# Order of the products in blocks two and three of the second MoE: two of layer one, then both halves of one of layer two

## The chip, the cores and the metric

One Trainium2 chip, one core. The metric is the device time of one execution in microseconds; the three runs of the kernel before took 2061.57 to 2063.62 us, with a median of 2063.37.

## What is computed

Sliding-window attention (4 x 8 heads, 576 positions, head size 64), then two feed-forward stages over the 2304 tokens of 512 values. The second one is the place of the change. Eight experts each have two layers, and their results are added with weights P that a Sinkhorn iteration over the gate's logits gives:

```python
for e in range(E):                      # E = 8, D = 512, F = 1024
    h = np.maximum(x @ w1[e], 0.0)      # layer one
    ye = h @ w2[e]                      # layer two
    out += P[:, e:e + 1] * ye
```

## The kernel before

The second MoE takes the tokens in three blocks of 768, each of two halves of 384 columns (HALF). Both layers are done as 2 x 2 block products with Strassen's scheme, seven products in place of eight, on sums and differences of the blocks. Every factor is split into a high and a low part, and a product of blocks is six matmuls with 384 moving columns (two parts of the contraction, and in each high x high, high x low, low x high; lines 122 to 124, the function mm3).

Blocks two and three run in one loop over m, from NQ = 16 to total - 1 = 47. I call one m a quad: it is half of an expert's F for one block, worked on as two pairs of slices of 128, so 16 quads make a block. A quad has 14 steps s; step(m, s) issues product p = s % 7 of layer one for pair s // 7 (g_product) and one half of a product of layer two of the quad before (y_product(m - 1, s): product s // 2, half dt = s % 2). In the texts g0 to g6 are the layer-one products of the first pair of a quad, g'0 to g'6 those of the second, and y is one half. Quad 16 has no layer-two products yet (old is false at m = 16; its first steps finish block one instead), quad 31's products of layer two follow a plain list of eight products (PLAIN), and those of quad 47 come after the loop, in last_quad. A manual schedule is declared ahead of this stage (line 859): every engine's work has the order in which the program issues it.

The seven products of layer one add up in three PSUM banks of a pair:

```python
    GP = [(0, "b11", 0), (1, "b21", 1), (5, "t2", 0), (4, "t1", 2), (6, "t3", 0), (2, "t4", 0), (3, "b22", 2)]
...
        o, b, bk = GP[p]
        first = p in (0, 1, 3)
```

The last number is the bank. With first a fresh bank is opened (one of four, in turn); otherwise the product adds onto what is there. Between two such products the bank's state is read out (g_evict): for p = 0 a ScalarE copy (line 939), p = 1 a VectorE sum (942), p = 2 a ScalarE copy (945), p = 4 a ScalarE copy called u3 and a VectorE sum with bank 2:

```python
            nc.scalar.copy(new_temp("u3", "m"), v1)
            c = v3 if inside else temps["u3"]
            nc.vector.tensor_add(c, v2, temps["u3"])
```

(lines 947 to 949), p = 5 a ScalarE Relu straight from the bank, p = 6 a VectorE sum (955). The results go through a Relu on ScalarE (line 1338) into R.

Layer two has four PSUM banks of its own, yb: two of them for each half dt. A product's result is added by VectorE to the sums acc in SBUF (line 1272, 128 x 384), before the next product on that bank.

Between these, step(m, s) issues for VectorE the scaling of R by the expert's weights (scaled, line 1212) and Strassen's sums (r_sum, lines 1217 to 1223), at s = 0 (t1), 2 (t3), 3 (t2), 5 (t4), and for ScalarE and GpSimd the splits in high and low parts (r_hi, line 1231; r_lo, line 1236), at s = 0, 2, 4, 5 and, for the next quad, 9, 12, 13. SP loads one weight block of layer one after each g product, in eight places (load_w1, line 763), and one of layer two at every odd step (w2_op, line 1248, nine places). x_switch changes the block's tokens at the end of a block.

Of the kernel before, what the change touches and what calls it, by code (L numbers as in the profile page):

```python
# [29 lines left out]
def attention_moe_moe2(  # L30
# [89 lines left out]
    def mm3(ps, lhs, rhs, first, last, **kw):  # L120
        (lh, ll), (rh, rl) = lhs, rhs
        nc.tensor.matmul(ps, lhsT=lh, rhs=rh, start=first, stop=False, **kw)  # L122
        nc.tensor.matmul(ps, lhsT=lh, rhs=rl, start=False, stop=False, **kw)  # L123
        nc.tensor.matmul(ps, lhsT=ll, rhs=rh, start=False, stop=last, **kw)  # L124
# [633 lines left out]
    def load_w1(j):  # L758

        n, p = divmod(j, 7)  # L760
        if NP <= n < NB * NP and j not in w1q:
            w = w1q[j] = p3.tile([P, 2, 2, P], F32R, name="w1o", tag="w1o", bufs=8)
            nc.sync.dma_start(raw(w), d_w1[n % NP][:, GP[p][0]])
# [160 lines left out]
    def g_product(n, p):  # L924
        o, b, bk = GP[p]
        first = p in (0, 1, 3)
        if first:
            gb[bk] = g_bank(f"g{bk}")
        w, x = slab[n][:, o] if n < NP else w1q.pop(7 * n + p), xop[b]
        for k in range(2):  # L930
            mm3(
                gb[bk][:, :HALF], (w[:, k, 0], w[:, k, 1]), (x[:, 0, k], x[:, 1, k]), first and k == 0, k == 1,
                skip_group_check=True,
            )

    def g_evict(p, rectify, inside=False):
        v1, v2, v3 = [gb[i][:, :HALF] if i in gb else None for i in (0, 2, 1)]
        if p == 0:
            nc.scalar.copy(new_temp("m1", "m"), v1)
        elif p == 1:  # L940
            c = v3 if inside else temps["m1"]
            nc.vector.tensor_add(c, v3, temps["m1"])
            rectify(c, 0, 0)
        elif p == 2:
            nc.scalar.copy(new_temp("u2", "u"), v1)
        elif p == 4:
# [3 lines that stand above are left out]
            rectify(c, 1, 1)  # L950
        elif p == 5:
            rectify(v1, 1, 0)
        elif p == 6:
            c = v2 if inside else temps["u2"]
            nc.vector.tensor_add(c, v2, temps["u2"])
            rectify(c, 0, 1)
# [15 lines left out]
    def x_switch(m, s):  # L972
        if m + 1 < NB * NQ and (m + 1) % NQ == 0:
            if s == 4:
                nc.vector.tensor_sub(xs["t1"], xs[0, 1], xs[0, 0])
            elif s == 6:
                nc.vector.tensor_sub(xs["t2"], xs[1, 1], xs["t1"])
            elif s == 8:
                nc.vector.tensor_sub(xs[0, 1], xs[1, 1], xs[0, 1])
            elif s == 11:  # L980
                nc.vector.tensor_sub(xs[1, 0], xs[1, 0], xs["t2"])
        elif m and m % NQ == 0 and s < 2:
            s += 14
        else:
            return
        order = LAST_SWITCH if m > NQ + 1 else SWITCH
        if s in order:
            nm, eng = order[s]
            src = {"b11": xs[0, 0], "b21": xs[1, 0], "b22": xs[1, 1], "t3": xs[0, 1], "t4": xs[1, 0]}.get(nm)
            x = xop[nm] = p2.tile([P, 2, 2, HALF], F32R, name=f"x{nm}", tag=f"x{nm}", bufs=1)  # L990
            split_sb(xs[nm] if src is None else src, x[:, 0], x[:, 1], (nc.vector, nc.gpsimd)[eng])
# [216 lines left out]
    def scaled(m, f, h):  # L1208

        pb = pbs[m // NQ, m % NQ // PER][:, h * HALF : (h + 1) * HALF]  # L1210
        r = R[m, f, h]
        nc.vector.tensor_mul(r, r, pb[:, None, :].to_broadcast([P, 2, HALF]))  # L1212

    def r_sum(m, nm):
        r = {(f, h): R[m, f, h] for f in range(2) for h in range(2)}
        if nm == "t1":
            nc.vector.tensor_sub(r[0, 0], r[0, 1], r[0, 0])  # L1217
        elif nm == "t2":
            nc.vector.tensor_sub(r[0, 0], r[1, 1], r[0, 0])
        elif nm == "t3":  # L1220
            nc.vector.tensor_sub(r[0, 1], r[1, 1], r[0, 1])
        elif nm == "t4":
            nc.vector.tensor_sub(r[1, 0], r[1, 0], r[0, 0])
# [14 lines left out]
    def r_op(m, nm):  # L1238
        r_hi(m, nm)
        if (m, nm) != (total - 1, "b21"):  # L1240
            r_lo(m, nm, nc.gpsimd)

    def w2_op(m, i):
        if m in PLAIN and i > 3:
            return
        o = (0, 2, 1, 3)[i] if m in PLAIN else YP[i][1]
        w = w2q[m, o] = wp.tile([P, 2, 2, 2 * P], F32R, name="w2o", tag="w2o", bufs=9)
        nc.sync.dma_start(raw(w), d_w2[m % NQ][:, o])

    def y_product(m, s):  # L1250

        i, dt = divmod(s, 2)
        b, op, bk, first, *dsts = (YP_LAST if m in PLAIN else YP)[i]
        if m < total - 1:
            bk %= 2
        ps = yb[2 * bk + dt]
        w, x = w2q[m, op], rop[m, b]
        ws = slice(dt * P, (dt + 1) * P)
        for a in range(2):
            mm3(  # L1260
                ps[:, :HALF], (w[:, a, 0, ws], w[:, a, 1, ws]), (x[:, 0, a], x[:, 1, a]), first and a == 0, a == 1,
                skip_group_check=True,
            )
        for dst in dsts:
            key = (m, dst, dt)
            if m % NQ == 0 and key not in touched:
                touched.add(key)
                if dt == 0:
                    acc[dst] = wp.tile([P, 2, HALF], F32, name=f"a{dst[0]}{dst[1]}", tag=f"a{dst[0]}{dst[1]}", bufs=1)
                nc.scalar.copy(acc[dst][:, dt], ps[:, :HALF])  # L1270
            else:
                nc.vector.tensor_add(acc[dst][:, dt], ps[:, :HALF], acc[dst][:, dt])  # L1272
# [54 lines left out]
    def step(m, s):  # L1327

        nonlocal wp
        if m < total:  # L1330
            pair, p = divmod(s, 7)

            def rectify(src, f, h):
                if pair == 0:
                    R[m, f, h] = (p3 if m % 2 else p2).tile(
                        [P, 2, HALF], F32, name=f"R{f}{h}", tag="Rb" if m % 2 else "Ra", bufs=4
                    )
                nc.scalar.activation(R[m, f, h][:, pair], src, AF.Relu)  # L1338

            g_product(2 * m + pair, p)  # L1340
            load_w1(7 * (2 * m + pair) + p + 8)
        old = NQ <= m - 1 < total
        if s in EARLY_OPS and m < total:
            scaled(m, *EARLY_OPS[s][1:])
        elif s in LATE_OPS and old and m < total:
            if s == 0:
                scaled(m - 1, 0, 1)
            if m - 1 not in PLAIN:
                r_sum(m - 1, LATE_OPS[s])
        if m < total:  # L1350
            g_evict(p, rectify)
        if s in EARLY_OPS and m < total:
            r_op(m, EARLY_OPS[s][0])
        elif s in LATE_SPLITS and old and m < total:
            if m - 1 not in PLAIN:
                r_op(m - 1, LATE_SPLITS[s])
            elif s == 2:
                r_op(m - 1, "t3")
        if old:
            if m - 1 not in PLAIN:  # L1360
                y_product(m - 1, s)
            else:
                for x in (s,) if s < 12 else (2 * s - 12, 2 * s - 11):
                    y_product(m - 1, x)
        if m < total:
            x_switch(m, s)
            if m > NQ:
                if s % 2:
                    w2_op(m, s // 2)
            elif s < 6:  # L1370
                values(before, (s,))
            elif s == 6:
                wps.close()
                wp = ctx.enter_context(tc.tile_pool(name="wpb", bufs=1))
            elif s % 2:
                for i in range(4) if s == 7 else (s // 2,):
                    w2_op(m, i)
            if s == 4 and m % PER == PER - 1 and m + 1 < total:
                load_pb((m + 1) // NQ, (m + 1) % NQ // PER)
        for d in range(2):  # L1380
            blk, q = divmod(m - d, NQ)
            if q == 0 and blk > 1:
                for dst, at in WHOLE:
                    for x in range(2):
                        if at + x == s + 14 * d:
                            turn_out(blk - 1, dst, x, yb[x] if dst == (1, 0) else None)
# [41 lines left out]
```

## Time and profile before

| | |
|---|---|
| median of three runs | 2063.37 us |
| lowest and highest run | 2061.57, 2063.62 us |
| span of the profiled execution | 2061.8 us |
| PE busy | 2025.9 us (98%) |
| VectorE busy | 1385.8 us (67%) |
| GpSimd busy | 1080.9 us (52%) |
| ScalarE busy | 955.5 us (46%) |
| DMA | 523.84 MB, 254 GB/s in the mean |

The page gives the span of the profiled execution and no other time for it; it lies 1.6 us under the median of the runs. In the timeline a matmul's start is recorded, its end is modelled, so consecutive matmuls overlap in the rows and the distance between starts is what counts.

### The profile page before, as it was taken

The numbers are of one execution on the slowest core, as the hardware profiler recorded it, in microseconds if no ns is written. First come the engines' busy times: TensorE is split into PE (matmuls) and PEld (weight loads), VectorE is DVE, ScalarE is ACT, GpSimd is POOL, SyncE is SP. The second block draws the span as 40 slices with busy tenths as digits, with TensorE's granted clock in tenths as the row PEclk, the third lists the DMA queues.
The fourth block names the chain that finished last, engine by engine and source line by source line (L and its number), as shares of the span: only waits on it lengthen the run. The fifth ranks groups of instructions, "written<-read, shape, count | busy, mean of one in ns | idle before, by whom it ended". The sixth has DMA issues, their size and how long they took to land.

```text
span 2061.8 us, 31510 instructions
## 1 busy us (share of the span) xinstructions
PE 2025.9 (98%) x10869; PEld 1854.1 (90%) x10869; DVE 1385.8 (67%) x2469; ACT 955.5 (46%) x1950; POOL 1080.9 (52%) x836
## 2 busy tenths in 40 slices
PE   7989999999999999999999999999999999999999
PEld 5767777887888899999999999999999999999999
DVE  7986755535147887777786766776676577667765
ACT  7665655434244444444444434444444444444443
POOL 4224343434358788788785444544454454445442
PEclk9999999999999999999999999999999999999999
DMA  7877877656649878887879878777786787877773
GB/s 208 280 211 252 265 221 195 193 164 204 209 159 327 295 307 319 320 310 287 313 297 343 285 254 256 259 259 256 253 273 228 260 256 260 258 256 235 270 260 106
DMA packets 290653, 523.84 MB, mean 254 GB/s; under 512 B 90416, under 2 KB 135104, under 8 KB 286400
## 3 DMA queue, kind: packets, MB, share of 16 engines
q1 hardware_dynamic: 290496, 521.85, 75.9%
q8 instruction: 87, 1.43, 0.3%
q14 instruction: 70, 0.57, 0.1%
HBM read 369.12 MB, written 152.64 MB: 253 GB/s over the span
## 4 chain that ended last, share of the span: by engine, by line
PE 69%; DVE 4%; issue 1%; ACT 1%; POOL 1%; DMA 0%; ACTq 0%; POOLq 0%; DVEq 0%
PE y L123 11%; PE y L124 11%; PE y L122 11%; PE g L122 11%; PE g L124 11%; PE g L123 11%; PE acc L122 1%; PE acc L123 1%; PE acc L124 1%; PE h L123 1%; PE h L122 1%; PE h L124 1%; DVE s L737 1%; DVE s L739 0%; DVE o L1044 0%
## 5 line engine op out<-in xcount | busy, mean ns | idle before, releaser
L1236 POOL TENSOR_TENSOR rb<-R,rb 128x768 fp32r<-128x768 f32 x95 | 214.0, 2253 | 345.3 <-ACT rb L1231 321.6
L1272 DVE TENSOR_TENSOR a<-y,a 128x384 f32<-128x384 f32 x420 | 232.4, 554 | 192.5 <-PE y L124 192.5
L1236 POOL TENSOR_TENSOR rt<-R,rt 128x768 fp32r<-128x768 f32 x121 | 230.4, 1915 | 138.5 <-ACT rt L1231 59.4
L114 POOL TENSOR_TENSOR w2a<-r,w2a 128x1024 fp32r<-128x1024 f32 x64 | 154.2, 2410 | 66.9 <-ACT w2a L113 66.9
L122 PE MATMUL g<-xt,w1o 128*128 128x384 f32 x512 | 173.8, 339 | 1.4 <-ACT u L947 1.0
L124 PE MATMUL g<-xt,w1o 128*128 128x384 f32 x512 | 172.6, 337 | 0.0
L123 PE MATMUL g<-xt,w1o 128*128 128x384 f32 x512 | 172.3, 337 | 0.0
L122 PE MATMUL y<-rt,w2o 128*128 128x384 f32 x496 | 168.1, 339 | 0.1
L123 PE MATMUL y<-rt,w2o 128*128 128x384 f32 x496 | 168.0, 339 | 0.0
L124 PE MATMUL y<-rt,w2o 128*128 128x384 f32 x496 | 167.4, 337 | 0.0
L1231 ACT ACTIVATE rt<-R 128x768 fp32r<-128x768 f32 x122 | 102.7, 842 | 134.7 <-DVE R L1217 84.0
L114 POOL TENSOR_TENSOR gl<-r,gh 128x512 fp32r<-128x512 f32 x64 | 83.0, 1297 | 155.9 <-ACT gh L113 130.9
L124 PE MATMUL y<-w2a,rl 128*128 128x512 f32 x384 | 150.1, 391 | 0.0
L123 PE MATMUL y<-w2a,rh 128*128 128x512 f32 x384 | 149.6, 390 | 0.2 <-POOL w2a L114 0.2
L122 PE MATMUL y<-w2a,rh 128*128 128x512 f32 x384 | 149.5, 389 | 0.0
L1212 DVE TENSOR_TENSOR R<-R,pb 128x768 f32<-128x768 f32 x128 | 138.5, 1083 | 5.4 <-ACT R L1338 3.9
L122 PE MATMUL y<-rb,w2o 128*128 128x384 f32 x408 | 138.3, 339 | 0.6 <-DVE a L1272 0.6
L123 PE MATMUL y<-rb,w2o 128*128 128x384 f32 x408 | 138.3, 339 | 0.0
L124 PE MATMUL y<-rb,w2o 128*128 128x384 f32 x408 | 137.6, 337 | 0.0
L122 PE MATMUL g<-xb,w1o 128*128 128x384 f32 x384 | 129.9, 338 | 0.0
L124 PE MATMUL g<-xb,w1o 128*128 128x384 f32 x384 | 129.5, 337 | 0.0
L123 PE MATMUL g<-xb,w1o 128*128 128x384 f32 x384 | 129.3, 337 | 0.0
(261 smaller groups left out, 5773.2 us busy)
## 6 DMA issues: line engine op xcount, KB each, us to landing
w1o<-d_w SPq DMA_DIRECT2D x448, 256.0 KB, 3.0
w2o<-d_w SPq DMA_DIRECT2D x218, 512.0 KB, 3.9
d_w<-w1a SPq DMA_DIRECT2D x32, 1792.0 KB, 11.6
d_w<-w2a SPq DMA_DIRECT2D x30, 1536.0 KB, 7.9
r<-in_moe_w_dram SPq DMA_DIRECT2D x64, 512.0 KB, 4.3
a<-d_in SPq DMA_DIRECT2D x48, 512.0 KB, 3.8
b<-d_out SPq DMA_DIRECT2D x48, 512.0 KB, 3.9
u<-in_moe_w_in_dram SPq DMA_DIRECT2D x16, 512.0 KB, 5.0
```

Of the source, the lines that this page charges most:

```text
L114: (eng or nc.gpsimd).tensor_sub(lo, src, raw(hi))
L122: nc.tensor.matmul(ps, lhsT=lh, rhs=rh, start=first, stop=False, **kw)
L123: nc.tensor.matmul(ps, lhsT=lh, rhs=rl, start=False, stop=False, **kw)
L124: nc.tensor.matmul(ps, lhsT=ll, rhs=rh, start=False, stop=last, **kw)
L737: nc.vector.tensor_sub(w1s[n][:, 2], w1s[n][:, 1], a11)
L1212: nc.vector.tensor_mul(r, r, pb[:, None, :].to_broadcast([P, 2, HALF]))
L1231: nc.scalar.activation(x[:, 0], R[m, f, h], AF.Copy)
L1236: eng.tensor_sub(x[:, 1], R[m, f, h], raw(x[:, 0]))
L1272: nc.vector.tensor_add(acc[dst][:, dt], ps[:, :HALF], acc[dst][:, dt])
```

## The change

In the loop over quads a step no longer issues one half of a layer-two product each time. At even s it issues none, at odd s both halves, s - 1 and s, of one product. For the quad with the plain list (m - 1 = 31) it is the same up to s = 11, and the last four halves come together at s = 13. Everything else in a step keeps its place.

```diff
--- before.py
+++ after.py
@@ -1356,12 +1356,13 @@
                 r_op(m - 1, LATE_SPLITS[s])
             elif s == 2:
                 r_op(m - 1, "t3")
-        if old:
+        if old and s % 2:
             if m - 1 not in PLAIN:
-                y_product(m - 1, s)
+                ys = (s - 1, s)
             else:
-                for x in (s,) if s < 12 else (2 * s - 12, 2 * s - 11):
-                    y_product(m - 1, x)
+                ys = (s - 1, s) if s < 12 else range(12, 16)
+            for x in ys:
+                y_product(m - 1, x)
         if m < total:
             x_switch(m, s)
             if m > NQ:
```

## Rows read from the trace of the kernel before

**Rows 1.** The page: its head, busy time of the engines, and weight loads to landing.

```profile
span 2061.8 us, 31510 instructions
...
PE 2025.9 (98%) x10869; PEld 1854.1 (90%) x10869; DVE 1385.8 (67%) x2469; ACT 955.5 (46%) x1950; POOL 1080.9 (52%) x836
...
w1o<-d_w SPq DMA_DIRECT2D x448, 256.0 KB, 3.0
```

**Rows 2.** Busy time by stretch (columns in the first line), blocks two and three.

```profile
core 0: us, PE busy (x) PEld busy (x) DVE busy (x) ACT busy (x) POOL busy (x), PEclk, DMA share, GB/s
1116.00:1562.00 446.00, 444.88 (x2526) 443.60 (x2526) 317.65 (x417) 189.75 (x328) 223.48 (x109) 1.00 0.80 263
1562.00:1600.00 38.00, 37.70 (x223) 36.89 (x222) 18.61 (x24) 18.86 (x36) 16.90 (x9) 1.00 0.70 226
1600.00:2037.00 437.00, 437.00 (x2487) 436.83 (x2486) 303.02 (x406) 183.78 (x317) 210.32 (x104) 1.00 0.77 251
```

**Rows 3.** Waits of PE, 1115.2 to 2037: engine, line, released by, us, times, longest.

```profile
PE y L122 <- DVE a L1272: 0.6, 1, 0.6
PE g L122 <- ACT u L947: 0.5, 1, 0.5
PE g L122 <- ACT m L939: 0.3, 1, 0.3
```

**Rows 4.** Timeline of PE, quad 16: start, us, engine, line, operation, operands, count, [idle before].

```profile
1108.22 0.33 PE L122 MATMUL g<-xt,w1o 128*128 128x384 f32 x1
...
1111.00 0.33 PE L123 MATMUL g<-xt,w1o 128*128 128x384 f32 x1
1111.17 0.34 PE L124 MATMUL g<-xt,w1o 128*128 128x384 f32 x1
1112.08 0.45 PE L122 MATMUL g<-xt,w1o 128*128 128x384 f32 x1 [0.57 <-ACT u L947]
1112.36 0.34 PE L123 MATMUL g<-xt,w1o 128*128 128x384 f32 x1
```

**Rows 5.** Timeline of PE, last quad: the first and last of 15 matmuls.

```profile
2041.34 0.33 PE L124 MATMUL y<-rb,w2o 128*128 128x384 f32 x1
...
2043.77 0.33 PE L123 MATMUL y<-rb,w2o 128*128 128x384 f32 x1
```

**Rows 6.** Timeline of ScalarE, quads 22 and 23, step s = 4.

```profile
1271.99 0.48 ACT L947 COPY u<-g 128x384 f32<-128x384 f32 x1 [0.65 <-PE g L124]
...
1300.01 0.85 ACT L1231 ACTIVATE rt<-R 128x768 fp32r<-128x768 f32 x1 [1.73 <-DVE R L1221]
1301.53 0.48 ACT L947 COPY u<-g 128x384 f32<-128x384 f32 x1 [0.67 <-PE g L124]
```

**Rows 7.** Timeline of ScalarE, quad 16, two copies from g's banks.

```profile
1107.43 0.48 ACT L939 COPY m<-g 128x384 f32<-128x384 f32 x1
...
1111.54 0.48 ACT L947 COPY u<-g 128x384 f32<-128x384 f32 x1
```

**Rows 8.** Timeline of PE, quad 23, around s = 4 (g, y, g).

```profile
1301.10 0.34 PE L124 MATMUL g<-xt,w1o 128*128 128x384 f32 x1
1301.28 0.33 PE L122 MATMUL y<-rt,w2o 128*128 128x384 f32 x1
...
1302.16 0.34 PE L124 MATMUL y<-rt,w2o 128*128 128x384 f32 x1
1302.34 0.34 PE L122 MATMUL g<-xt,w1o 128*128 128x384 f32 x1
```

**Rows 9.** Timeline of VectorE, quad 23, s = 0 to 4.

```profile
1293.94 2.42 DVE L1217 TENSOR_TENSOR R<-R,R 128x768 f32<-128x768 f32 x1
1296.29 0.54 DVE L1272 TENSOR_TENSOR a<-y,a 128x384 f32<-128x384 f32 x1
1296.76 0.54 DVE L942 TENSOR_TENSOR m<-g,m 128x384 f32<-128x384 f32 x1
1297.22 0.54 DVE L1272 TENSOR_TENSOR a<-y,a 128x384 f32<-128x384 f32 x1
1297.69 2.29 DVE L1221 TENSOR_TENSOR R<-R,R 128x768 f32<-128x768 f32 x1
1299.91 0.54 DVE L1272 TENSOR_TENSOR a<-y,a 128x384 f32<-128x384 f32 x1
1300.37 0.94 DVE L1219 TENSOR_TENSOR R<-R,R 128x768 f32<-128x768 f32 x1
```

## Prediction

> **What bounds the kernel now.** Read the head of the page first: PE is busy for 2025.9 of 2061.8 us, the other engines for at most two thirds [rows 1]. The stretches by time show where this matters for the change: over blocks two and three PE is busy for 444.88 of 446 us and for 437.00 of 437 us [rows 2]. The waits of PE over the same stretch come to three, 1.4 us together [rows 3]. So nothing that shortens another engine's work can move the end here; only two things can. One is the spacing of the matmuls themselves, the other a wait of PE that is not there now.
>
> The spacing is not the same everywhere. In quad 16 no layer-two product runs, and over 17 intervals from the matmul at 1108.22 to that at 1111.17 the spacing is 2.95 / 17 = 0.1735 us [rows 4]. At the end, where only layer two is left, it is (2043.77 - 2041.34) / 14 = 0.1736 us [rows 5]. In between, where the two kinds alternate, the same ScalarE copy comes again after 1301.53 - 1271.99 = 29.54 us [rows 6], one quad of 14 steps and 168 matmuls, so 0.1758 us each. Two steps, 24 matmuls, take 29.54 / 7 = 4.22 us where the even spacing would give 24 x 0.1735 = 4.164; the alternation costs 0.056 us in two steps, and two steps have four changes between the kinds.
>
> **The change, part by part.** Nothing is added or taken away: the same matmuls, evictions and loads are issued. In two steps PE did g, y, g, y and now does g, g, y, y. The 31 quads from 17 to 47 have it, 7 x 31 = 217 pairs of steps. SP's loads are issued at the same places of the program; a load of the first layer's weights is released by the g product that frees its place, and the second g of a pair ends one product earlier. With eight places and 3.0 us to landing [rows 1] that is hidden: eight places last for eight steps, 8 x 2.11 = 17 us.
>
> *Gain: fewer changes of kind.* Four changes in two steps become two. What a change costs is not shown by one row. The upper end is the whole excess, 217 x 0.056 = 12.2 us; the lower end is nothing, if the excess belongs to the stretch and not to the changes. A loss is excluded, since runs of one kind keep the even spacing at both places where the trace has them. I take half, 6 us, because half the changes go and the even spacing holds in the runs of either kind, next to the same evictions.
> The Trainium skill (TensorE: Matmul & The Clock Gate, "Back-to-back issue gap") gives a warm matmul the columns over 2.4 GHz plus 2.5 ns, an estimate of 162.5 ns for 384 columns, in which order plays no part; the rows have 173.5 and 175.8 ns, so it doesn't describe them. By it this gain would be 0 and the sum 6 us higher.
>
> *Cost: a wait that the y half covered.* The parts of g go to three PSUM banks of a pair, and p = 2, 4 and 5 add onto the bank that p = 0 opened. Ahead of each addition the state of the bank must have been copied out by ScalarE. Go through the new order with that in mind: (g0 g1) yy (g2 g3) yy (g4 g5) yy (g6 g'0) yy (g'1 g'2) yy (g'3 g'4) yy (g'5 g'6) yy. Between g0 and g2, g2 and g4, g'0 and g'2, g'2 and g'4 lie three products, between g'4 and g'5 two; p = 6, which adds onto the bank that the eviction of p = 4 reads, is three behind it. One product is cover enough: in quad 16 only g'1 lies between g'0 and g'2, the copy runs from 1107.43 for 0.48 us, and g'2 starts without a wait at 1108.22 [rows 4, 7]. One place has none: g5 comes directly after g4, in every quad. The copy u3 that g5 waits for had a y half of 1.06 us to hide behind; now it has nothing.
>
> The trace of before has this very sequence once, in quad 16, where g'5 follows g'4 without anything between. The last matmul of g'4 starts at 1111.17, the copy runs from 1111.54 for 0.48 us, and the next matmul starts at 1112.08 where 1111.34 was due, then the one behind it 0.28 us later in place of 0.17 [rows 4, 7]. That is 0.74 + 0.11 = 0.85 us, and only the 0.57 us of it that are shown as idle are named a wait. In quad 23 the copy for s = 4 starts at 1301.53, the last matmul of g4 at 1301.10 [rows 6, 8], 0.43 us apart where quad 16 has 0.37. So the copy for g5 will end 0.06 us later, and the price is 0.85 to 0.91 us. ScalarE is free ahead of it (0.67 us idle [rows 6]) and what it did last, the high part of t3, waits for a sum on VectorE whose place among the y additions moves by nothing that counts. I take 0.90 x 31 = 27.9 us; the ends are 0.85 x 31 = 26.4 and 0.91 x 31 = 28.2.
>
> *VectorE, out of step with PE.* The two y additions of a pair now stand behind the g eviction and the sum of both steps. VectorE is already late here: around s = 0 it needs 2.42 and 2.29 us for two sums, and the addition of a y half waits in its queue [rows 9]. Who waits for an addition? The next y product on the same bank, and that was and stays two g products and one y half away. Counted in quad 23: the sum t3 ends at 1299.98, t2 (0.94 us) now goes directly behind it, then the first addition of product 1 ends at about 1301.5. The next product on that bank (t1) would start at 1302.34 and, behind the new wait, at 1303.2. Cover 1.7 us, so nothing. The scaled R and the splits that belong to odd steps only come earlier, as their g does. The operands r of layer two are wanted later by one product in the first half. Nothing.
>
> *Single places.* The three waits of 1.4 us and what follows them lie around the turn of block two to three; g'5 there has more cover now, VectorE's splits collide anew. I put this at 0, with 1.5 us to either side.
>
> **Sum.** 27.9 - 6.0 = +21.9 us, on the profiled span of 2061.8: 2083.7. The median of the runs is 2063.4, 1.6 above that span, so 2085.3; I say 2085. With the ends of all terms: 26.4 - 12.2 - 1.5 = +12.7, 2076; 28.2 + 1.5 = +29.7, 2093.
>
> **Rivals.**
> - *The wait at g5 stays out, and the fewer changes are kept.* That would be so if PE's queue held a y half between g4 and g5 after all, because the build orders this place otherwise than the program; then the change does not do at s = 4 and 5 what it says, and 2063.4 - 6.0 = 2057 remains. Against it: a manual schedule is declared ahead of this stage (line 859), and in quads 16 and 23 the order of the trace is that of the program [rows 4, 8]. It decides at the gain: the wait would have to stay under 6.0 / 31 = 0.19 us a quad for any time to be saved, under 0.39 if all of the 12.2 us is gained, and the copy alone takes 0.48. Chance 0.04 for a time saved, and 0.04 for a part of the wait that cancels the gain, at 2063.
> - *VectorE becomes the second bound.* The additions of both halves end up behind 2.4 us sums, and the product that wants their bank waits as well, or ScalarE waits for a late sum and the copy u3 with it. Priced at one addition, 0.54 us [rows 9], in each quad: 16.7 us more, 2102. Against it are the 1.7 us of cover counted above. Chance 0.08.
> - *The spacing belongs to the stretch, not to the order.* No gain, 2091; it lies inside the forecast's range and shares its chance.
>
> **How the numbers follow.** Forecast 0.84, over 2076 to 2093. The range of 2075 to 2094 takes in this and leaves out the two other cases, 0.16 together. A measurement here can tell about 0.2% (4 us) from no change. Slower by more: 0.84 + 0.08 = 0.92. Within: 0.04. Faster: 0.04.
>
> **What would show it.** In the profile of the changed kernel PE should have a wait on ScalarE, line 947, at the first matmul of g, 31 times at some 0.6 us shown as idle, and no other new row among its waits. The period of the copy at L947 should grow from 29.54 to about 30.2 us. Two steps without the wait should take 4.19 us; 4.22 would say that the order is worth nothing. If line 947 isn't among the waits, the step about g5 is wrong. If PE waits for L1272 or for rt and rb, the one about VectorE is.

## The result and the profile after

The changed kernel takes 2086.62 us in the median (2085.54 to 2087.33) beside 2063.22 us of the kernel before on the same chip: a ratio of 1.0113, with a 95% interval of 1.0102 to 1.0125. It is slower, by 23.4 us. The forecast was 2085.

The head of the page of the changed kernel, the line for [rows 1]:

```profile
span 2085.0 us, 31382 instructions
...
PE 2031.0 (97%) x10869; PEld 1850.6 (89%) x10869; DVE 1373.8 (66%) x2469; ACT 954.2 (46%) x1950; POOL 1040.0 (50%) x836
```

PE has about the same work (2031.0 us), the span is 23.2 us longer. Where PE lost it is said by the stretches (columns as in [rows 2]) and by PE's waits (as in [rows 3]) of the changed kernel:

```profile
1116.00:1562.00 446.00, 436.63 (x2465) 431.34 (x2464) 301.89 (x407) 184.40 (x320) 194.41 (x105) 1.00 0.81 260
...
1600.00:2037.00 437.00, 427.98 (x2422) 423.34 (x2421) 288.85 (x394) 179.71 (x312) 187.03 (x101) 1.00 0.80 249
```

```profile
PE g L122 <- ACT u L947: 19.0, 30, 0.9
```

PE now is idle for 9.4 and 9.0 us in the two long stretches, where it was idle for 1.1 and 0.0. One row is left of the waits: 30 in this window, one in each of quads 17 to 46, all on the copy of line 947. (Quad 47's lies behind it.) The three single waits of [rows 3] are gone. The place itself, in the timeline of PE and then of ScalarE, is shown for quad 23; the first row is that of the y half two steps earlier, and of ScalarE the copies of quads 16 and 22 stand ahead, for comparison with [rows 6, 7, 8]:

```profile
1298.31 0.33 PE L122 MATMUL y<-rb,w2o 128*128 128x384 f32 x1
...
1302.52 0.33 PE L122 MATMUL y<-rb,w2o 128*128 128x384 f32 x1
...
1303.59 0.33 PE L122 MATMUL y<-rb,w2o 128*128 128x384 f32 x1
...
1304.63 0.34 PE L122 MATMUL g<-xt,w1o 128*128 128x384 f32 x1
...
1305.51 0.34 PE L124 MATMUL g<-xt,w1o 128*128 128x384 f32 x1
1306.48 0.44 PE L122 MATMUL g<-xt,w1o 128*128 128x384 f32 x1 [0.62 <-ACT u L947]
1306.76 0.34 PE L123 MATMUL g<-xt,w1o 128*128 128x384 f32 x1
```

```profile
1110.88 0.48 ACT L947 COPY u<-g 128x384 f32<-128x384 f32 x1
...
1275.56 0.48 ACT L947 COPY u<-g 128x384 f32<-128x384 f32 x1 [1.07 <-PE g L124]
...
1304.03 0.85 ACT L1231 ACTIVATE rt<-R 128x768 fp32r<-128x768 f32 x1 [1.81 <-DVE R L1221]
1305.94 0.48 ACT L947 COPY u<-g 128x384 f32<-128x384 f32 x1 [1.07 <-PE g L124]
```

The last matmul of g4 starts at 1305.51, the copy runs from 1305.94 to 1306.42, and g5 starts at 1306.48: 0.97 us after g4's last matmul in place of 0.17, and its second matmul is 0.28 us behind in place of 0.17. The wait is 0.80 + 0.11 = 0.91 us. A quad takes 1305.94 - 1275.56 = 30.38 us, where [rows 6] give 29.54: 0.84 more. So 0.91 us was lost in a quad and 0.07 us at most came back by the fewer changes of kind. ScalarE was free ahead of the copy, as forecast: 1.07 us idle behind the split of t3.

The executions differ by some us ahead of the change, in code that is the same. To keep that out I also give the time from the second copy of quad 16 at line 947 (1111.54 in [rows 7], 1110.88 here) to the end of the span: 950.3 us before, 974.1 after, +23.9.

### The profile page after: what moved, and what is told of

Same layout as the page of the kernel before. It is cut to its first block, busy times and chain, and to the rows that moved or that the text cites. A ratio compares the mean times of both kernels' runs of the same rounds, so it can differ in the third digit from the quotient of the medians.

```text
span 2085.0 us, 31382 instructions
## 1 busy us (share of the span) xinstructions
PE 2031.0 (97%) x10869; PEld 1850.6 (89%) x10869; DVE 1373.8 (66%) x2469; ACT 954.2 (46%) x1950; POOL 1040.0 (50%) x836
## 4 chain that ended last, share of the span: by engine, by line
PE 70%; DVE 3%; ACT 1%; issue 1%; POOL 0%; DMA 0%; ACTq 0%; SPq 0%; POOLq 0%; DVEq 0%
PE y L124 11%; PE y L122 11%; PE y L123 11%; PE g L122 11%; PE g L124 11%; PE g L123 11%; ACT u L947 1%; PE acc L122 1%; PE acc L123 1%; PE acc L124 1%; PE h L123 1%; PE h L122 1%; PE h L124 1%; DVE s L737 1%; DVE s L739 0%
## 5 line engine op out<-in xcount | busy, mean ns | idle before, releaser
L1236 POOL TENSOR_TENSOR rb<-R,rb 128x768 fp32r<-128x768 f32 x95 | 178.8, 1883 | 360.5 <-PE y L124 183.6
L1272 DVE TENSOR_TENSOR a<-y,a 128x384 f32<-128x384 f32 x420 | 228.2, 555 | 160.0 <-PE y L124 159.8
L1236 POOL TENSOR_TENSOR rt<-R,rt 128x768 fp32r<-128x768 f32 x121 | 224.0, 1862 | 186.7 <-ACT rt L1231 186.7
L1212 DVE TENSOR_TENSOR R<-R,pb 128x768 f32<-128x768 f32 x128 | 162.9, 1274 | 26.0 <-ACT R L1338 26.0
```

The costliest lines, as they stand in the source:

```text
L1236: eng.tensor_sub(x[:, 1], R[m, f, h], raw(x[:, 0]))
```

## The experiments

| run | order of y, or edit | median us | ratio, interval | one quad, us | copy of quad 16 to end |
|---|---|---|---|---|---|
| before | y behind every g | 2063 | 1 | 29.54 | 950.3 |
| after | pairs | 2086.62 | 1.0113 (1.0102 to 1.0125) | 30.38 | 974.1 |
| e1_g5_covered | pairs but at s = 4, 5 | 2059.64 | 0.9987 (0.9978 to 0.9995) | 29.50 | 947.5 |
| e2_only_g5 | a pair at s = 4, 5 alone | 2088.73 | 1.0132 (1.0118 to 1.0145) | 30.44 | 978.3 |
| e7_copy_twice | after, copy u3 doubled | 2103.2, one run | | 30.90 | 990.0 |
| e3_long_runs | 8 changes of kind in a quad | 2109.8 | 1.0226 (1.0213 to 1.0240) | 31.09 | 996.7 |
| e5_ten_changes | 10 changes | 2088.62 | 1.0124 (1.0107 to 1.0141) | 30.34 | 976.4 |
| e6_twelve_changes | 12 changes | 2063.7 | 1.0008 (0.9999 to 1.0017) | 29.44 | 952.0 |
| e4_moving | e1, y's tokens as g's | 2056.03, one run | | 29.41 | 945.0 |
| e4_weights | e1, y's weights as g's | 2057.44, one run | | 29.39 | 947.7 |
| e4_both | e1, both as g's | 2047.89, one run | | 29.12 | 937.8 |
| e8_one_region | e1, other places in SBUF | 2048.81 | 0.9931 (0.9917 to 0.9944) | 29.12 | 936.3 |
| e9_old_order | before, places as in e8 | 2050.93 | 0.9941 (0.9928 to 0.9955) | 29.12 | 938.6 |
| e10_r_low | e1, r low, the rest high | 2056.93, one run | | 29.39 | 944.1 |

The quad is quad 23 in every run, from the copy at s = 4 of quad 22 to that of quad 23 on ScalarE's timeline. Each ratio is to the kernel before on the same chip.

### Is the wait of g5 the whole loss?

The change is undone at one of seven places, or made at that place alone. The lines that matter are:

```diff
 e1_g5_covered, against the changed kernel
-        if old and s % 2:
-            if m - 1 not in PLAIN:
+        if old and (s % 2 or s == 4):
+            if s in (4, 5):
+                ys = (s,)
+            elif m - 1 not in PLAIN:
                 ys = (s - 1, s)
...
 e2_only_g5, against the kernel before
+            if s in (4, 5):
+                ys = (4, 5) if s == 5 else ()
```

> The change everywhere but at s = 4 and 5, where g and y alternate as before. Theory (the wait of g5 for the copy u3 is the whole loss): no wait on line 947 in quads 17 to 47, a quad takes 6 x 4.21 + 4.22 = 29.5 us, and the median is that of the kernel before less 1.4 us for fewer changes of kind and less some 2 us at the turn of the blocks: 2060 (2058 to 2063). Rival (pairing as such costs, by VectorE's bunched additions or otherwise): the time stays above 2075.

> The kernel before with the change at s = 4 and 5 alone. Theory: 31 waits of 0.90 us, 27.9 us, and next to no gain elsewhere: 2091 (2089 to 2092). Rival (the loss is spread over the pairs): about a seventh of 23 us, 2067.

e1_g5_covered takes 2059.64 us, e2_only_g5 2088.73, which is 0.3 us under the range expected for it. ScalarE's timeline and PE's waits of e1_g5_covered, then the same two of e2_only_g5:

```profile
1109.72 0.48 ACT L947 COPY u<-g 128x384 f32<-128x384 f32 x1
...
1271.02 0.48 ACT L947 COPY u<-g 128x384 f32<-128x384 f32 x1 [1.07 <-PE g L124]
...
1300.52 0.48 ACT L947 COPY u<-g 128x384 f32<-128x384 f32 x1 [1.05 <-PE g L124]
```

```profile
PE y L122 <- DVE a L1272: 0.8, 1, 0.8
```

```profile
1108.34 0.48 ACT L947 COPY u<-g 128x384 f32<-128x384 f32 x1
...
1273.27 0.48 ACT L947 COPY u<-g 128x384 f32<-128x384 f32 x1 [0.67 <-PE g L124]
...
1303.71 0.48 ACT L947 COPY u<-g 128x384 f32<-128x384 f32 x1 [0.67 <-PE g L124]
```

```profile
PE g L122 <- ACT u L947: 19.4, 31, 0.9
PE y L122 <- DVE a L1272: 0.6, 1, 0.6
PE g L122 <- ACT m L939: 0.3, 1, 0.3
```

With g5 covered no wait on line 947 is left, and the six other pairs lose nothing: a quad of 29.50 us. With the pair at s = 4 and 5 alone a quad takes 30.44, that is 0.90 more than before, and from the copy of quad 16 to the end it is 978.3 - 950.3 = 28.0 us more, 31 x 0.90 = 27.9. (Its 31 waits on line 947 in this window are those of quads 17 to 46 and the single one of [rows 3].) A loss spread over the pairs would have left e1_g5_covered above 2075 and e2_only_g5 near 2067; only the wait of g5 fits. The 2.8 us by which e1_g5_covered is below the kernel before (947.5 against 950.3) are 30 x 0.04 = 1.2 in the quads, and the rest, 1.6, is mainly the balance of two single places. At the turn of the blocks, from the copy at s = 4 of quad 31 to that of quad 32, it takes 29.70 us where the kernel before takes 32.09, and all three single waits of [rows 3] are gone; about 1.0 us of that is lost again in quad 17, by the one wait that e1_g5_covered has:

```profile
1123.16 0.44 PE L122 MATMUL y<-rt,w2o 128*128 128x384 f32 x1 [0.79 <-DVE a L1272]
```

Then the copy's length, as the one thing that the wait should follow. Behind the copy of line 947 the same one is issued again, `nc.scalar.copy(temps["u3"], v1)`, in blocks two and three.

> The changed kernel with the copy u3 issued twice in a row on ScalarE, wherever it reads a bank of blocks two and three. Theory (g5 waits for the copy's end): the wait of 0.90 us grows by one copy, 0.45 to 0.48 us, a quad from 30.39 to 30.86 us, the whole to some 2101; at g'5, which has two y halves of cover, nothing. Rival (the wait is a fixed time between the engines and the copy's length doesn't matter): 30.39 and 2086.

ScalarE's timeline of e7_copy_twice, and PE's waits from 1115.2 us to the end, quad 47 with them:

```profile
1279.17 0.48 ACT L947 COPY u<-g 128x384 f32<-128x384 f32 x1 [1.07 <-PE g L124]
1279.68 0.48 ACT L949 COPY u<-g 128x384 f32<-128x384 f32 x1
...
1310.07 0.48 ACT L947 COPY u<-g 128x384 f32<-128x384 f32 x1 [1.07 <-PE g L124]
1310.58 0.48 ACT L949 COPY u<-g 128x384 f32<-128x384 f32 x1
```

```profile
PE g L122 <- ACT u L949: 35.2, 31, 1.1
```

Now PE waits for the second copy (line 949 of that kernel), and a quad takes 30.90 us, 0.52 more than after, with 0.51 us between the two copies' starts; that is a little over the 0.45 to 0.48 us expected. In the other pair, where two y halves cover g'5, no wait came up. The wait is for the end of the copy and as long as the copy makes it.

### Is there anything in longer runs of one kind?

The gain that I had expected of fewer changes between g and y came out small. Three more orders test whether it goes with the number of changes. What stands in the step is a table of the y halves behind a step's g, for the quads without the plain list. Its line in e3_long_runs, e5_ten_changes and e6_twelve_changes, in this order:

```diff
+                ys = {4: range(4), 8: range(4, 8), 11: range(8, 12), 13: (12, 13)}.get(s, ())
+                ys = {1: (0, 1), 3: (2, 3), 4: (4, 5), 11: range(6, 12), 13: (12, 13)}.get(s, ())
+                ys = {1: (0, 1), 3: (2, 3), 4: (4, 5), 8: (6, 7), 11: range(8, 12), 13: (12, 13)}.get(s, ())
```

> Runs of g and y that are longer: y halves 0 to 3 after g4, 4 to 7 after g'1, 8 to 11 after g'4, 12 and 13 after g'6, so 8 changes of kind in a quad where the kernel before has 28 and the changed one 14, and g5 never directly behind g4. Theory (each change costs 24 ns as in the changed kernel): a quad takes 168 x 0.1735 + 8 x 0.024 = 29.34 us, 0.2 less than before, 30 quads: 2057 (2055 to 2060). Rival one (the excess does not go with the changes): 2061 to 2063. Rival two (one y half between two products on one bank is too little for VectorE's addition): a new wait on line 1272 of some 0.3 us at up to six places of a quad, 2075 to 2110.

> Ten changes of kind in a quad, where e1_g5_covered has 16: y halves 0 and 1 after g1, 2 and 3 after g3, 4 and 5 after g4, 6 to 11 after g'4, 12 and 13 after g'6 (the quad with the plain list as in e1_g5_covered). Theory (24 ns a change, whatever the runs' length, and ScalarE's copies have cover at every place): a quad takes 168 x 0.1735 + 10 x 0.024 = 29.39 us, 0.11 less than in e1_g5_covered, 3.3 us over its quads: 2056 (2054 to 2058). Rival (the additions of the run of six y halves, with one half between two on one bank, come too late, or a ScalarE copy does, as at line 945 in e3_long_runs): a wait of 0.3 us or more in each quad, 2065 or above.

> As e5_ten_changes, but with y halves 6 and 7 after g'1, so that g'2 has two products of cover again: twelve changes of kind in a quad. Theory: no wait, a quad of 168 x 0.1735 + 12 x 0.024 = 29.44 us, against 29.50 in e1_g5_covered, 1.9 us less over the quads: 2058 (2056 to 2060). Rival: the wait at line 939, or another behind the late copies, stays with over 0.3 us a quad: 2067 or above.

e3_long_runs takes 2109.8, e5_ten_changes 2088.62 and e6_twelve_changes 2063.7 us, each above what the theory gave (2057, 2056 and 2058). PE's waits of the three, in this order:

```profile
PE g L122 <- ACT u L945: 40.9, 29, 1.5
PE y L122 <- DVE a L1272: 2.1, 2, 1.8
PE g L122 <- DMA w1o<-d_w: 1.8, 1, 1.8
```

```profile
PE g L122 <- ACT m L939: 18.8, 27, 1.5
PE y L122 <- DVE a L1272: 3.2, 2, 2.4
```

```profile
PE y L122 <- DVE a L1272: 3.9, 2, 3.7
PE g L122 <- DMA w1o<-d_w: 0.8, 1, 0.8
```

In the first two a run of five or seven g gets ahead of ScalarE: the copies of lines 945 and 939 come too late, for 1.5 us at the worst. Why they come late is seen on ScalarE's timeline of e3_long_runs at the start of a quad:

```profile
1302.95 0.48 ACT L939 COPY m<-g 128x384 f32<-128x384 f32 x1 [0.96 <-PE g L124]
1305.84 0.84 ACT L1231 ACTIVATE rt<-R 128x768 fp32r<-128x768 f32 x1 [2.41 <-DVE R L1217]
1306.59 0.51 ACT L1338 ACTIVATE R<-m 128x384 f32<-128x384 f32 x1
1307.00 0.46 ACT L945 COPY u<-g 128x384 f32<-128x384 f32 x1
```

The copy at 1307.00 is of a g that PE finished long before; ahead of it in ScalarE's queue is the split at 1305.84, which sat for 2.41 us on a VectorE sum (L1217), and the Relu behind it. I had put the danger on the additions of y (line 1272); in the quads it lies in g's own copies, behind a wait for another engine in the same queue. e6_twelve_changes has no such wait in the quads, and its quad of 29.44 us is the number expected (12 x 0.024 + 29.15); but at the turn of the blocks, where VectorE and ScalarE also prepare the next tokens, a y half waits for 3.7 us, early in quad 17 a g waits for 0.8 us for the load of its weights, and the time is that of the kernel before. So a change of kind costs 24 ns in runs of two and more, but each of these three orders loses elsewhere at least what it gains by it.

### What makes a change of kind cost 24 ns?

In the changed kernel's rows above the first y half behind two g takes 1303.59 - 1302.52 = 1.07 us and the second 1304.63 - 1303.59 = 1.04; over the quads the means are 1.065 and 1.040 us for y, and 1.068 and 1.041 for g. Three kernels in the order of e1_g5_covered let y read what g reads; then y's sums are others, while each product has the same six matmuls. In e4_moving `rop[m, b]` is `xop[b]` in y_product, in e4_weights the stationary operand is `w1q` of the next g, and e4_both has both.

> As e1_g5_covered, but y's moving operand is the block of tokens that g uses (xop) in place of r, up to the last quad; the split of r is still made and isn't read, so the sums of layer two are others. If the excess at a change of kind comes from the change of place of the moving operand, the products after a change take 1.041 us as the others do, and a quad 29.15 us; if not, 1.065 and 29.5.

> As e1_g5_covered, but the stationary operand of y is the layer-one block already loaded for the next g, in place of the layer-two block, up to the last quad; the loads of the layer-two blocks are still made. The sums of layer two are others. If the excess at a change of kind comes from where the stationary operand lies: products after a change take 1.041 us, a quad 29.15. If it needs the moving operand to change place, as e4_moving suggests: 1.065 and 29.5 stay.

> As e1_g5_covered, with both operands of y taken from where g has its own (tokens and layer-one block): only the PSUM banks differ between the kinds. If the excess of 24 ns and the uneven spacing of y in e4_moving both come from the operands' places in SBUF, every product takes 1.041 us and a quad 29.15; if the PSUM banks have a part in it, it stays above 29.3.

A quad takes 29.41, 29.39 and 29.12 us; the first two lie between the values named for them, 29.15 and 29.5. (The whole times of e4_weights and e4_both also hold a single wait of 3.1 and 2.7 us for a load in quad 17, so the quads are compared.) With both operands from g's places every product takes 1.04 us, although the PSUM banks still alternate; so the banks have no part in it. With one operand moved the excess only changes its form. PE's timeline of e4_moving, the first matmul of each of five products in a row:

```profile
1293.92 0.33 PE L122 MATMUL g<-xt,w1o 128*128 128x384 f32 x1
...
1294.96 0.33 PE L122 MATMUL g<-xt,w1o 128*128 128x384 f32 x1
...
1296.00 0.34 PE L122 MATMUL y<-xb,w2o 128*128 128x384 f32 x1
...
1297.06 0.34 PE L122 MATMUL y<-xb,w2o 128*128 128x384 f32 x1
...
1298.12 0.33 PE L122 MATMUL g<-xt,w1o 128*128 128x384 f32 x1
```

There g is even (1.04 and 1.04 us) and both y halves take 1.06.

What differs is either the place in SBUF or the way in which the operands are written. The next kernels keep all operands and change only places. In the build of the kernel before y's operands lie low in a partition (layer-two blocks at 27 to 64 thousand bytes, r at 64 to 113) and g's lie high (layer-one blocks at 142 to 159, tokens at 183 to 226).

```diff
 e8_one_region, against e1_g5_covered
+                p4 = ctx.enter_context(tc.tile_pool(name="p4", bufs=1, side="right"))
...
-        x = rop[m, nm] = wp.tile([P, 2, 2, HALF], F32R, name=f"r{nm}", tag=f"r{tag}", bufs=1)
+        x = rop[m, nm] = p4.tile([P, 2, 2, HALF], F32R, name=f"r{nm}", tag=f"r{tag}", bufs=1)
...
-        w = w2q[m, o] = wp.tile([P, 2, 2, 2 * P], F32R, name="w2o", tag="w2o", bufs=9)
+        w = w2q[m, o] = p4.tile([P, 2, 2, 2 * P], F32R, name="w2o", tag="w2o", bufs=9)
...
-                    R[m, f, h] = (p3 if m % 2 else p2).tile(
+                    R[m, f, h] = (wp if m % 2 else p2).tile(
```

e9_old_order has these places and the step of the kernel before. e10_r_low is as e8_one_region, but r stays in wp, behind the places for the last tokens.

> The order of e1_g5_covered and the same work; only places in SBUF change. The operands of y (r and the layer-two blocks) lie at 27 to 114 thousand bytes of a partition before, those of g at 142 to 226 thousand; here r and the layer-two blocks are put right below the layer-one blocks, 75 to 155 thousand, and R of the odd quads goes to the low end. Theory (the excess is one of the operands' places): it changes, and falls where both operands of y come near to those of g: a quad between 29.12 and 29.45 us, 2048 to 2058. Rival (it is not the place but that the operands are others, or were written by others): 29.50 and the time of e1_g5_covered, 2059.6.

> The order of the kernel before (a y half behind every g) with the places of e8_one_region. Theory (the order costs nothing by itself, the excess is all of the places): a quad of 29.12 us as in e8_one_region, 30 x 0.42 = 12.6 us less than before: 2049 to 2051, the two microseconds at the turn of the blocks apart. Rival (28 changes of kind cost something at any place): above 29.2 us a quad.

> The order of e1_g5_covered; the layer-two blocks lie at 118 to 155 thousand bytes, close to those of layer one, and r alone stays low: b11, b22, b21 at 46 to 64 thousand, t1 at 64 to 70, t3, t2, t4 at 86 to 107. If it is the moving operand's place, and there is a limit near 65 thousand, then the products with b11, b21, b22 and the g behind them have the excess and those with t3, t2, t4 have none, about 29.3 us a quad. If the layer-two blocks' old place alone did it: none, 29.12. If the distance between the two moving operands counts: all have it, 29.5.

ScalarE's timeline of e8_one_region and of e9_old_order, and PE's of e10_r_low (the first matmul of two y, two g and the next y):

```profile
1111.07 0.48 ACT L947 COPY u<-g 128x384 f32<-128x384 f32 x1
...
1270.42 0.48 ACT L947 COPY u<-g 128x384 f32<-128x384 f32 x1 [0.93 <-PE g L124]
...
1299.54 0.48 ACT L947 COPY u<-g 128x384 f32<-128x384 f32 x1 [0.94 <-PE g L124]
```

```profile
1110.88 0.47 ACT L947 COPY u<-g 128x384 f32<-128x384 f32 x1
...
1269.82 0.48 ACT L947 COPY u<-g 128x384 f32<-128x384 f32 x1 [0.52 <-PE g L124]
...
1298.94 0.48 ACT L947 COPY u<-g 128x384 f32<-128x384 f32 x1 [0.53 <-PE g L124]
```

```profile
1280.94 0.33 PE L122 MATMUL y<-rt,w2o 128*128 128x384 f32 x1
...
1281.99 0.34 PE L122 MATMUL y<-rt,w2o 128*128 128x384 f32 x1
...
1283.03 0.34 PE L122 MATMUL g<-xt,w1o 128*128 128x384 f32 x1
...
1284.10 0.33 PE L122 MATMUL g<-xt,w1o 128*128 128x384 f32 x1
...
1285.14 0.33 PE L122 MATMUL y<-rt,w2o 128*128 128x384 f32 x1
```

With the operands of y next to those of g the excess is gone in both orders: 29.12 us a quad, 168 x 0.1733. e8_one_region takes 2048.81 us, 0.9931 of the kernel before (0.9917 to 0.9944), and is the fastest version here that keeps y's own operands; e9_old_order, with y behind every g, is at 0.9941 (0.9928 to 0.9955), and the intervals overlap. So with these places the order is worth nothing in the quads. e10_r_low, with only r left low, has 1.05 us for the first y and 1.07 for the first g behind a change, the second ones 1.04; and it has them alike for t3, t2 and t4 at 86 to 107 thousand and for b11, b21 and b22 at 46 to 64. The limit near 65 thousand that I had thought possible isn't there, and with r low again most of the excess is back (29.39 of 29.50). R of the odd quads and the sums acc were at other places in these kernels too, but the excess does not hang on them: e4_weights, where they and r (64 to 113 thousand) lie as in the kernel before, has the same spacings behind a pair as e10_r_low (1.05, 1.04 and 1.07 us) and the same quad of 29.39, and only y's moving operand sets it apart from e4_both with its 29.12. Which addresses, or which distance between the two, the chip minds, these runs do not settle: r was harmless at 112 to 155 thousand (e8_one_region), and not at 46 to 107 (e10_r_low) or 64 to 113 (e4_weights). What in the chip makes it is open as well.

## Why the prediction was right, step by step

**What bounds the kernel.** Right. PE sets the time, and both the loss and the later gains came from PE's waits and the spacing of its matmuls; e8_one_region takes 13 us less than the kernel before on its chip (2061.81) with the same work on every other engine.

**The wait of g5.** Right in place, number and size. Forecast were 0.85 to 0.91 us at 31 places, read from quad 16, where the sequence already stood once; measured were 0.91 in the changed kernel and 0.90 in e2_only_g5, where it stands alone. The 0.06 us by which ScalarE's copy starts later at s = 4 than in quad 16 were there too (0.43 us behind the last matmul).

**Fewer changes of kind.** Here the term was mis-sized: 6.0 us forecast, and 0.05 to 0.07 us a quad measured, some 1.6 to 2.2 us over 31 quads. The failed step is "I take half, 6 us, because half the changes go": the excess didn't halve. Four changes in two steps cost 0.056 us, 14 ns each; in pairs the two that are left cost 24 ns each, 0.048 us together. Why a change costs less where single products alternate, no run shows. The sign named for it says the same: two steps without the wait take 1302.52 - 1298.31 = 4.21 us in the changed kernel, where 4.19 was forecast and 4.22 was to mean that the order is worth nothing; and the period grew to 30.38 us, not to about 30.2. That the sentence on the Trainium skill's rule (TensorE: Matmul & The Clock Gate, "Back-to-back issue gap"), by which this gain is 0, came nearer is no support for it: no run has the spacing of 162.5 ns that it starts from (173.3 ns in e8_one_region), and a change of kind does cost time where the operands lie apart. The excess is one of the operands' places and not of the order as such, which the prediction had not thought of.

**VectorE.** Right: no wait on line 1272 came up in the changed kernel. The longer runs show that a late VectorE can hold PE where more g stand together; in the quads this came by ScalarE's copies, and by the additions only at single places.

**Single places.** Put at 0 with 1.5 us to either side; the three waits of 1.4 us went, and from the copy of quad 16 to the end the loss is 23.9 us, where 31 waits less the gain in the quads would be 28 - 2 = 26. So some 2 us came back elsewhere, just outside the margin, and ScalarE's timeline has them at the turn of the blocks: from the copy at s = 4 of quad 31 to that of quad 32 the kernel before takes 1569.94 - 1537.85 = 32.09 us, 2.55 over its usual quad, and the changed one 1579.62 - 1549.04 = 30.58, 0.20 over. This and the smaller gain have opposite signs (4 us less gained in the quads, 2 us more at the turn), so the sum of 21.9 came out 1.5 us under the 23.4 measured. That the forecast of 2085 lies so near 2086.62 is in part luck: the wait was known to 0.1 us, and two errors of 4 and 2 us partly cancelled.

**The rivals.** That the wait stays out is refuted by the 30 rows of it. That VectorE becomes the second bound did not happen in this order. The third, no gain because the spacing belongs to the stretch, came near in size, but its reason is not the one: in the same stretch every product takes 1.04 us once the operands lie elsewhere (e8_one_region).

## What to carry to other kernels

Before two products are put side by side on a bound engine, go through the new order and look for a pair in which the second adds onto a bank that another engine must first read: what looked like filler between them was the cover of that read, and here six pairs of seven were harmless and one cost 0.9 us each time. Look for a stretch of the same program in which the sequence already stands; it has the price. And when a stream of matmuls has an uneven spacing, try where its operands lie before trying their order.

## What was not expected of the hardware

The spacing of the matmuls depends on where their operands lie in SBUF. With y's operands at 27 to 113 thousand bytes of a partition and g's at 142 to 226 thousand, the six matmuls behind a change between them take 1.07 us in place of 1.04 when the runs are two products long; with y's operands at 75 to 155 thousand, right below g's, all take 1.04 (a quad of 29.12 us against 29.50 in the same order). With tokens and layer-two blocks apart within one product (e4_moving) every y product takes 1.06 us. Also, a wait of 0.9 us in each quad did not cost PE its clock: it stayed at the higher level of 2.4 GHz (granted 1.00 in both long stretches of the changed kernel).
